# A windowed-attention and MLP kernel: the fallback path moved off VectorE, the guard's flag computed earlier, and the last tile's first store issued by SyncE

## The chip, the cores and the metric

The kernel runs on one core of a Trainium2 chip. The metric is the device time of one execution in microseconds, as the median of several runs; lower is better. One more execution is taken with the hardware profiler. Engines are named as the profile names them: PE (TensorE), PEld (its weight loads), DVE (VectorE), ACT (ScalarE), POOL (GpSimd), SP (SyncE). A q behind an engine's name (ACTq) marks what its sequencer does itself: waits, branches, register loads, DMA issues.

## The reference

Two stages: attention with four sink keys and a window of 128, then a normalised two-layer MLP with a residual.

```python
# q, k, v: (4, 8, 768, 64); n_sink = 4, window = 128
scores = (q @ k.T) / sqrt(64)
keep = (key < n_sink) | (0 <= query - key < window)
a = softmax(where(keep, scores, -1e9))         # the row maximum is taken off first
x = (a @ v).transpose(0, 2, 1, 3).reshape(4, 768, 512)
xn = (x - mean(x)) / sqrt(var(x) + 1e-6) * g_ln
out = x + maximum(xn @ w_ch1, 0) @ w_ch2       # 512 -> 2048 -> 512, float32
```

## The kernel before

The 4 x 768 rows are 24 tiles of 128 rows, taken in 12 chunks of two tiles. A chunk's q and k are brought into transposed layout (through PE for the first chunks, by transposing DMAs on SP for later ones), the scores of a key block against the query block are made in PSUM, ACT takes their exponential (L685, L740), DVE multiplies by a 0/1 mask (L744), and PE multiplies by v with a column of ones, so that the row sums come out beside the values (L774). DVE takes the reciprocal of the sums into the tile rec (L787), scales (L789) and makes the statistics (L793, L795, L797); POOL makes 1/sqrt(var) (L802, L803). The MLP of a chunk is 64 matmuls into four PSUM banks with ReLU by ACT (L843, L853), then 16 matmuls for each of its two tiles (L872), an add of the residual on DVE (L880) and a store of the tile (L884). The last tile's product is made in two halves of 256 columns, each with an add and a store of its own: the first half's store is issued by ACT, the second half's by SP.

The order is not written by hand. A planner (class Plan) gets every piece of work as P.op with an engine, a modelled cost and a due time, and simulates the engines; the instructions are then emitted in the order of the modelled start times. On PE, pieces with a due time above 40 are taken strictly by it. The MLP of chunk c is due from 16c + 8 on; the products of the last chunk's tiles have due times 192.5 to 195.5 in steps of one for the second last tile (four groups of four matmuls), and from 196.5 on for the last one.

The fast path leaves the row maximum out, which holds as long as no row sum leaves a wide range. A guard checks that: three DVE operations clamp rec, compare, and count the deviations into n_bad (L906 to L908); PE adds the count up over the partitions with one small float32 matmul (gsum, L911, due 196.2); DVE casts the result into the integer tile flag (L913). After all planned work every engine loads the flag into a register (L941), and each branches on it (L942): if it is above zero, the function general computes everything again with the row maximum taken off; otherwise each engine jumps over its part of that code to the end of the program. There SP waits for all DMA queues and all engines, and a barrier over the five engines ends the program (L977). With these inputs the flag is zero and general does not run.

general (L232 to L355) is a loop over the four batches with the six row blocks written out. Its softmax runs mainly on DVE: maxima, subtractions, sums, reciprocal, multiplications; so do the statistics and the last add.

Of the kernel before, what the change touches and what calls it, by code (L numbers as in the profile page):

```python
# [9 lines left out]
AF = mybir.ActivationFunctionType  # L10
ALU = mybir.AluOpType
# [186 lines left out]
def pe(us):  # L198
    return {"PE": (us, us + Plan.PE_DRAIN)}
# [26 lines left out]
NEVER = -1e9  # L226
# [5 lines left out]
def general(tc, nc, slots, pairs, ones, ident_f, ident, w1, w2, mhalf, g_s, g_r, q, k, v, out, scale):  # L232


    V, A, G, T, DMA = nc.vector, nc.scalar, nc.gpsimd, nc.tensor, nc.gpsimd.dma_start
    B, H, S, D = q.shape
    RB, HP, NS, DM = S // 128, H // 2, g_s.shape[2], H * D
    f32 = {n: [t.bitcast(FP32) for t in slots[n]] for n in ("kT", "qT", "kts", "pe")}
# [5 lines left out]
    sc = [t.rearrange("p a b c -> p (a b c)").rearrange("p (h c) -> p h c", h=4) for t in slots["natf"]]  # L244
    aT = [[flat(f32["pe"][2 * i + a]) for a in range(2)] for i in range(3)]
    xs, os_, xn, xnt, h1 = slots["ot"][0:2], slots["ot"][2:4], slots["xc"][0], slots["xnt"][0], slots["h1"]
    mx, sm = g_r[:, 0, :], g_r[:, 1, :]

    def transposes(src, dst):
# [4 lines left out]
    with tc.For_i(0, B, 1) as b:  # L254
# [5 lines left out]
        for r in range(RB):  # L260
            x, cur, prev = xs[r % 2], r % 2, (r + 1) % 2
# [4 lines left out]
            transposes(k_n, kT[cur])  # L266
            if r == 0:
                for t in sc:
                    V.memset(t[:, :, 0:128], NEVER)
            for a in range(HP):  # L270
                s_ps = pairs[a % 2]
                for h2 in range(2):
# [20 lines left out]
                if r < 2:  # L293
                    A.copy(sink, g_s[:, 4 * i:4 * i + 4, :])
            if r < 2:
                V.memset(g_s, NEVER)
            X = mybir.AxisListType.X
            V.tensor_reduce(out=mx, in_=g_s, op=ALU.max, axis=X)
            for i, t in enumerate(sc):
                V.tensor_reduce(out=g_r[:, 2, 4 * i:4 * i + 4], in_=t, op=ALU.max, axis=X)  # L300
            V.tensor_tensor(mx, mx, g_r[:, 2, :], op=ALU.max)
            for t, m in ((g_s, mx), (sc[0], mx[:, 0:4]), (sc[1], mx[:, 4:8])):
                V.tensor_tensor(t, t, m.unsqueeze(2).to_broadcast(list(t.shape)), op=ALU.subtract)
                A.activation(t, t, AF.Exp)
            V.tensor_reduce(out=sm, in_=g_s, op=ALU.add, axis=X)
            for i, t in enumerate(sc):
                V.tensor_reduce(out=g_r[:, 2, 4 * i:4 * i + 4], in_=t, op=ALU.add, axis=X)
            V.tensor_tensor(sm, sm, g_r[:, 2, :], op=ALU.add)
            V.tensor_scalar(sm, sm, 1e-9, None, op0=ALU.add)
            V.reciprocal(sm, sm)  # L310
            for t, m in ((g_s, sm), (sc[0], sm[:, 0:4]), (sc[1], sm[:, 4:8])):
                V.tensor_tensor(t, t, m.unsqueeze(2).to_broadcast(list(t.shape)), op=ALU.mult)
            for a in range(2):
                for i, rows in ((0, 128), (1, 128), (2, NS)):
                    for h in range(4):
# [11 lines left out]
                    T.matmul(ones[3][:, ds], lhsT=l, rhs=m, start=n == 0, stop=n == len(use) - 1)  # L327
            A.copy(x, ones[3])
            st = slots["st"][r % 2]
            V.bn_stats(st[:, 8:14], x)  # L330
            V.bn_aggr(st[:, 14:16], st[:, 8:14])
            G.tensor_scalar(st[:, 17:18], st[:, 15:16], 1e-6, None, op0=ALU.add)
            G.tensor_tensor(st[:, 16:17], st[:, 17:18], mhalf, op=ALU.pow)
            V.tensor_scalar(xn, x, st[:, 14:15], st[:, 16:17], op0=ALU.subtract, op1=ALU.mult)
            pb = ones[0].bitcast(BF16)
            for j in range(4):
                T.transpose(pb[:, 128 * j:128 * j + 128], xn[:, 128 * j:128 * j + 128], ident)
# [10 lines left out]
            for i in range(2):  # L348
                for ht in range(16):
                    at = 256 * (ht % 2) + 128 * i  # L350
                    T.matmul(ones[2 + i], lhsT=h1[ht // 2][:, at:at + 128], rhs=w2[ht // 4][:, ht % 4, :],
                             start=ht == 0, stop=ht == 15)
                V.tensor_tensor(os_[i], ones[2 + i], xs[i], op=ALU.add)
                at = 128 * (r - 1 + i)
                DMA(out[b, at:at + 128, :], os_[i])  # L355

# [2 lines left out]
def kernel(  # L359
# [12 lines left out]
    nc = tc.nc  # L372

    B, H, S, D = q.shape
    NS = int(n_sink)
# [3 lines left out]
    DM = moe_w_ch1.shape[0]  # L379
# [4 lines left out]
    NC = B * RC  # L384
# [7 lines left out]
    P = Plan()  # L392
# [6 lines left out]
    ones = [psum.tile([128, 512], FP32, name=f"one{i}") for i in range(4)]  # L399
# [31 lines left out]
    junk = const("junk", [128, 512], BF16)  # L431
    rec, low = const("rec", [128, NT, H], FP32), const("low", [128, NT, H], FP32)
    n_bad, flag = const("n_bad", [128, 1], FP32), const("flag", [1, 1], mybir.dt.int32)
    g_s, g_r = const("g_s", [128, H, NS], FP32), const("g_r", [128, 3, H], FP32)
    ones_f = const("ones_f", [128, 1], FP32)
    mhalf, one_e = const("mhalf", [128, 1], FP32), const("one_e", [128, 2], FP32)
# [10 lines left out]
    V, G = nc.vector, nc.gpsimd  # L447
# [377 lines left out]
    def mlp(c):  # L825
        T = 16.0 * c + 8.0
        xnt = xnt_b[c]
        h1 = []
        by_tile = c < PAR["by_tile"]
        for u in range(NH1 // 2):  # L830
            ph, hb = Buf(f"ph{c}_{u}", "one"), Buf(f"h{c}_{u}", "h1")

            def mm_t(e, u=u, ph=ph):
                for s in range(4):
                    for j in range(NDM):
                        nc.tensor.matmul(ph.t[:, 128 * s:128 * s + 128], lhsT=w1[u // 2][:, j, 128 * s:128 * s + 128],  # L836
                                         rhs=xnt.t[:, j, 128 * (u % 2):128 * (u % 2) + 128], start=j == 0, stop=j == NDM - 1)

            def mm(e, u=u, ph=ph):
                for s in range(2):  # L840
                    ht = 2 * u + s
                    for j in range(NDM):
                        nc.tensor.matmul(ph.t[:, 256 * s:256 * s + 256],  # L843
                                         lhsT=w1[ht // 4][:, j, 128 * (ht % 4):128 * (ht % 4 + 1)],
                                         rhs=xnt.t[:, j, :], start=j == 0, stop=j == NDM - 1)
            pr = T + u + 0.5
            o = P.op(f"ph{c}_{u}", pe(0.944 if by_tile else 0.872), pr, mm_t if by_tile else mm, reads=[xnt_t[2 * c + u % 2] if by_tile else xnt, (Bw1 if c < PAR["x_by_dma"] else Bw1g)[u // 2]],
                     writes=[ph], hold=[hb, xnt])
            last_use[u // 2] = [o]

            def rl(e, ph=ph, hb=hb):
                if e == "ACT":
                    nc.scalar.activation(hb.t, ph.t, AF.Relu)  # L853
                else:
                    V.tensor_scalar_max(hb.t, ph.t, 0.0)
            P.op(f"rl{c}_{u}", {"ACT": act(512), "DVE": dve(512)}, pr - 3, rl, reads=[ph], writes=[hb])
            h1.append(hb)
        T += 8
        for i in range(2):
            t = 2 * c + i  # L860
            b, r = t // RB, t % RB
            ot, st, rs, x = Buf(f"ot{t}", "ot"), xst_b[t], xst_b[t, "rs"], x_b[t]
            parts = 2 if t == NT - 1 else 1
            wd = DM // parts
            for f in range(parts):
                pc = Buf(f"pc{t}{f}", "one")
                sl = slice(wd * f, wd * (f + 1))
                for s in range(4):
                    def mm(e, s=s, i=i, pc=pc, sl=sl, wd=wd):
                        for ii in range(4):  # L870
                            ht = 4 * s + ii
                            nc.tensor.matmul(pc.t[:, 0:wd],  # L872
                                             lhsT=(h1[2 * s + i].t[:, 128 * ii:128 * ii + 128] if by_tile else
                                                   h1[ht // 2].t[:, 256 * (ht % 2) + 128 * i:256 * (ht % 2) + 128 * i + 128]),
                                             rhs=w2[s][:, ii, sl], start=ht == 0, stop=ht == NH1 - 1)
                    P.op(f"pc{t}{f}_{s}", pe(0.865 / parts), T + 4 * i + s + 2 * f + 0.5, mm,
                         reads=[*([h1[2 * s + i]] if by_tile else h1[2 * s:2 * s + 2]), Bw2[s]], **({"writes": [pc]} if s == 0 else {"rw": [pc]}))
                oo = Buf(f"oo{t}{f}")
                P.op(f"o{t}{f}", {"DVE": dve(wd, 1.14)}, T + 4 * i + 3.5, lambda e, sl=sl, pc=pc, wd=wd, ot=ot, st=st, x=x:
                     V.scalar_tensor_tensor(ot.t[:, sl], in0=pc.t[:, 0:wd], scalar=st.t[:, 16:17],  # L880
                                            in1=x.t[:, sl], op0=ALU.mult, op1=ALU.add),
                     reads=[pc, st, rs, x], writes=[ot, oo])
                P.op(f"st{t}{f}", {"ACT" if parts == 2 and not f else "SP": (0.35, 0.4)}, T + 4 * i + 3.6,
                     lambda e, sl=sl, ot=ot, b=b, r=r: (nc.sync if e == "SP" else nc.scalar).dma_start(  # L884
                         out[b, 128 * r:128 * (r + 1), sl], ot.t[:, sl]),
                     reads=[ot, oo], dma=HW_S)
# [18 lines left out]
    def guard(e):  # L905
# [2 lines left out]
        V.tensor_reduce(out=n_bad, in_=low, op=ALU.add, axis=mybir.AxisListType.XY)  # L908
    nb_b, pt_f, fl_b = Buf("n_bad"), Buf("ptf", "one"), Buf("flag")
    P.op("guard", {"DVE": fix(0.9)}, 1000.0, guard, reads=recs, writes=[nb_b])  # L910
    P.op("gsum", pe(0.06), 16.0 * NC + 4.2, lambda e: nc.tensor.matmul(  # L911
        pt_f.t[0:1, 0:1], lhsT=n_bad, rhs=ones_f, start=True, stop=True), reads=[nb_b, Bc["ones_f"]], writes=[pt_f])
    P.op("gflag", {"DVE": fix(0.1)}, 1000.0, lambda e: V.tensor_copy(flag, pt_f.t[0:1, 0:1]),  # L913
         reads=[pt_f], writes=[fl_b])
# [4 lines left out]
    t = 1.2  # L919
    for o in order:  # L920
# [5 lines left out]
        if n > 0 and o.start - t > 0.6:  # L926
            free = [(max([e_ for b_, e_ in banks[i].lives if b_ < t], default=0.0), i) for i in range(8)
                    if all(e_ < t or b_ > o.start + 0.3 for b_, e_ in banks[i].lives)]
            if free:
                i = min(free)[1]  # L930
# [51 lines left out]
```

## Time and profile before

| what | us |
|---|---|
| median of three runs (221.90, 222.38, 223.41) | 222.38 |
| the profiled execution's own time | 222.43 |
| its span, first to last instruction | 220.8 |
| PE busy / DVE busy / ACT busy / POOL busy | 212.1 / 117.2 / 108.8 / 89.8 |
| granted TensorE clock, mean | 0.998 |
| last matmul group begins, takes | 212.78, 3.61 |
| last add on DVE begins, takes | 216.49, 0.48 |

How to read it: the span counts from the first instruction of the profiled execution to the last; the execution's own time is 1.6 us longer, which lies around it. "Busy" leaves out waits, branches, register loads and DMA issues; these appear only as queue rows (ACTq and so on), with their duration in ns and the start of the first and last in us from the span's start. In the chain of waits a row is a start, a length and the work that held the end back. A TENSOR_LOAD is the load of the flag into an engine's register, a COMPARE_BRANCH the branch on it, an EVENT_SEMAPHORE a wait or a signal.

### The profile page before, as it was taken

The numbers are of one execution on the slowest core, as the hardware profiler recorded it, in microseconds if no ns is written. First come the engines' busy times: TensorE is split into PE (matmuls) and PEld (weight loads), VectorE is DVE, ScalarE is ACT, GpSimd is POOL, SyncE is SP. The second block draws the span as 40 slices with busy tenths as digits, with TensorE's granted clock in tenths as the row PEclk, the third lists the DMA queues.
The fourth block names the chain that finished last, engine by engine and source line by source line (L and its number), as shares of the span: only waits on it lengthen the run. The fifth ranks groups of instructions, "written<-read, shape, count | busy, mean of one in ns | idle before, by whom it ended". The sixth has DMA issues, their size and how long they took to land.

```text
span 220.8 us, 5072 instructions
## 1 busy us (share of the span) xinstructions
PE 212.1 (96%) x2033; PEld 144.6 (65%) x2033; DVE 117.2 (53%) x269; ACT 108.8 (49%) x163; POOL 89.8 (41%) x130
## 2 busy tenths in 40 slices
PE   6888999999999999999999999999999999999991
PEld 2556975764964964964955965965955955966861
DVE  5499745585796725725706815716706706722011
ACT  3767565145546447445546546445545546531700
POOL 7987663798073480760460741740110110120000
PEclk9999999999999999999999999999999999999999
DMA  5999999999999896999997997998713511111012
GB/s 158 160 184 206 177 207 193 155 211 149 175 171 141 137 146 110 149 127 119 143 124 119 143 118 121 130 123 111 129 38 80 136 28 47 59 39 72 23 52 62
DMA packets 108576, 27.45 MB, mean 124 GB/s; under 512 B 99201, under 2 KB 105601, under 8 KB 108545
## 3 DMA queue, kind: packets, MB, share of 16 engines
q0 software_dynamic: 74944, 13.11, 79.6%
q1 hardware_dynamic: 32400, 13.28, 29.4%
q10 hardware_dynamic: 1200, 0.66, 1.1%
q8 instruction: 18, 0.29, 0.6%
q14 instruction: 14, 0.11, 0.1%
HBM read 27.30 MB, written 6.29 MB: 152 GB/s over the span
## 4 chain that ended last, share of the span: by engine, by line
PE 90%; DVE 4%; DMA 2%; ACT 1%; issue 1%; DVEq 0%
PE one L872 39%; PE one L843 35%; PE pair L726 5%; PE pair L774 4%; PE one L836 2%; DMA natf<-in_k_dram 2%; PE pair L769 1%; DVE st L793 1%; DVE x L789 1%; PE one L632 1%; PE one L576 1%; PE one L730 1%; PE pair L665 1%; DVE xnt L821 1%; DVE xc L797 1%
## 5 line engine op out<-in xcount | busy, mean ns | idle before, releaser
L872 PE MATMUL one<-w,h 128*128 128x512 bf16 (+1 forms) x400 | 89.0, 371 | 0.0
L853 ACT ACTIVATE h<-one 128x512 bf16<-128x512 f32 x95 | 56.8, 598 | 59.3 <-PE one L843 54.2
L843 PE MATMUL one<-xnt,w 128*128 128x256 bf16 x704 | 82.4, 273 | 0.0
L843 PEld LDWEIGHTS <-w 128*128 128x128 bf16 x704 | 67.4, 98 | 10.2
L872 PEld LDWEIGHTS <-h 128*128 128x128 bf16 x400 | 37.4, 98 | 38.6 <-issue 2.0
L744 DVE TENSOR_TENSOR pe<-pe,mask 128x1024 bf16<-128x1024 bf16 (+1 forms) x40 | 26.0, 650 | 55.6 <-ACT pe L740 54.7
L740 ACT ACTIVATE pe<-pair 128x1024 bf16<-128x1024 f32 (+1 forms) x40 | 36.2, 957 | 34.1 <-PE pair L726 31.8
L618 POOL DMA_DIRECT2D nat<-in_k_dram x16 | 14.3, 893 | 39.6 <-DMA kT<-nat 29.7
L880 DVE SCALAR_TENSOR_TENSOR ot<-one,st,x 128x512 f32<-128x512 f32 (+1 forms) x25 | 18.2, 726 | 22.6 <-PE one L872 22.4
L802 POOL TENSOR_SCALAR st<-st 128x1 f32<-128x1 f32 x24 | 7.5, 313 | 43.2 <-DVE st L795 42.1
L541 POOL DMA_DIRECT2D vn<-in_v_dram x24 | 21.9, 920 | 3.7 <-DMA w<-in_moe_w_ch_dram 3.1
L618 POOL DMA_DIRECT2D nat<-in_q_dram x16 | 14.8, 926 | 11.7 <-DMA qT<-nat 8.5
L793 DVE BATCH_NORM_STATS2 st<-x 128x6 f32<-128x512 bf16 x24 | 16.7, 695 | 0.8
L774 PEld LDWEIGHTS <-pe 128*128 128x128 bf16 x352 | 14.0, 97 | 2.3 <-ACT pe L685 0.6
L803 POOL TENSOR_TENSOR st<-st,mhalf 128x1 f32<-128x1 f32 x24 | 14.2, 593 | 2.0
L789 DVE TENSOR_TENSOR x<-pair,rec 128x512 bf16<-128x512 f32 x20 | 13.8, 691 | 0.7
L726 PEld LDWEIGHTS <-kT 64*128 64x128 bf16 x216 | 6.9, 94 | 8.5 <-issue 8.3
L774 PE MATMUL pair<-vn,pe 128*128 128x65 bf16 x296 | 12.2, 193 | 0.0
L726 PE MATMUL pair<-qT,kT 64*128 64x128 bf16 (+1 forms) x216 | 11.6, 238 | 0.0
L797 DVE TENSOR_SCALAR xc<-x,st 128x512 bf16<-128x512 bf16 x24 | 9.1, 377 | 0.9
L787 DVE RECIPROCAL rec<-pair 128x8 f32<-128x8 f32 x20 | 4.1, 204 | 9.9 <-PE pair L774 9.9
L685 ACT ACTIVATE pe<-pair 128x1024 bf16<-128x1024 f32 (+1 forms) x8 | 7.2, 918 | 3.6 <-PE pair L679 3.6
(84 smaller groups left out, 123.3 us busy)
## 6 DMA issues: line engine op xcount, KB each, us to landing
out_dram<-ot SPq DMA_DIRECT2D x23, 256.0 KB
w<-in_moe_w_ch_dram POOLq DMA_DIRECT2D x8, 512.0 KB, 12.3
vn<-in_v_dram POOLq DMA_DIRECT2D x24, 128.0 KB, 6.1
nat<-in_k_dram POOLq DMA_DIRECT2D x22, 128.0 KB, 5.8
nat<-in_q_dram POOLq DMA_DIRECT2D x22, 128.0 KB, 5.0
natf<-in_k_dram SPq DMA_DIRECT2D x2, 256.0 KB
natf<-in_q_dram ACTq DMA_DIRECT2D x2, 256.0 KB
xnt<-xc SPq DMA_TRANSPOSE x18
```

The costliest lines, as they stand in the source:

```text
L541: P.op(f"vld{t}", {"POOL": (0.87, 0.9)}, prio, lambda e: G.dma_start(bv.t[:, :, 0:64], v[b, :, 128 * r:128 * (r + 1), :].rearrange("h p d ...
L618: lambda e, nat=nat, ap=ap: G.dma_start(nat.t, ap), writes=[nat], dma=SW)
L726: nc.tensor.matmul(pp.t[:, h2, col:col + q1 - q0], lhsT=kt.t[rs, hp, k0:k0 + 128], rhs=qT.t[rs, hp, q0:q1], start=i == 0, stop=True, skip_ ...
L740: P.op(f"ex{c}{hp}", {"ACT": act(2 * n)}, d + 0.1 + 0.05 * j, lambda e, pp=pp, pb=pb: nc.scalar.activation(pb.t[:, :, 0:n], pp.t[:, :, 0:n ...
L744: V.tensor_mul(pb.t[:, :, 0:n], pb.t[:, :, 0:n], mm),
L774: nc.tensor.matmul(bank(h // 4)[:, 65 * (h % 4):65 * (h % 4) + 65], lhsT=part(h, n), rhs=vn_b[tv].t[:, h, :], start=(not R and h % 4 == 0 ...
L789: P.op(f"x{t}{run[0]}", {"DVE": dve(512 * share)}, dd + 0.11, lambda e, pv=pv, rc=rc, run=run: V.tensor_tensor(x.t[:, 256 * run[0]:256 * r ...
L793: P.op(f"bn{t}", {"DVE": fix(0.60)}, d + 0.12, lambda e: V.bn_stats(st.t[:, 8:14], x.t), reads=[x], writes=[st, mv])
L843: nc.tensor.matmul(ph.t[:, 256 * s:256 * s + 256], lhsT=w1[ht // 4][:, j, 128 * (ht % 4):128 * (ht % 4 + 1)], rhs=xnt.t[:, j, :], start=j ...
L853: nc.scalar.activation(hb.t, ph.t, AF.Relu)
L872: nc.tensor.matmul(pc.t[:, 0:wd], lhsT=(h1[2 * s + i].t[:, 128 * ii:128 * ii + 128] if by_tile else h1[ht // 2].t[:, 256 * (ht % 2) + 128 ...
L880: V.scalar_tensor_tensor(ot.t[:, sl], in0=pc.t[:, 0:wd], scalar=st.t[:, 16:17], in1=x.t[:, sl], op0=ALU.mult, op1=ALU.add),
```

## The change

In general, DVE keeps the maxima and the reciprocal. Fills, subtractions, multiplications and the additions of the small sums go to POOL; the row sums and the statistics are made by ACT with an accumulating output, with POOL for the small steps; the last add becomes a copy by ACT and an add by POOL. In the planned part two things change: gsum is due at 192.7 instead of 196.2, and the first half's store of the last tile is issued by SP. All lines from L232 on are higher by up to six in the changed file.

By the built programs' instruction lists, three things move in the planned part. On PE the small matmul stands behind the first four of the second last tile's 16 matmuls instead of behind all 16. On DVE the cast of the flag stands ahead of that tile's add instead of behind it, with one wait instruction fewer. On SP the flag's load stands ahead of that tile's store, and both halves' stores are the last two before the branch; on ACT the flag's load follows the last activation directly. Behind the branch DVE has 34 rows instead of 128, ACT 185 instead of 155, POOL 168 instead of 92; PE and SP keep theirs.

```diff
@@ general
+    junk = f32["pe"][8].rearrange("p a b -> p (a b)")[:, 0:256]
...
-                    V.memset(t[:, :, 0:128], NEVER)
+                    G.memset(t[:, :, 0:128], NEVER)
...
-                V.memset(g_s, NEVER)
+                G.memset(g_s, NEVER)
...
-                V.tensor_tensor(t, t, m.unsqueeze(2).to_broadcast(list(t.shape)), op=ALU.subtract)
+                G.tensor_tensor(t, t, m.unsqueeze(2).to_broadcast(list(t.shape)), op=ALU.subtract)
                 A.activation(t, t, AF.Exp)
-            V.tensor_reduce(out=sm, in_=g_s, op=ALU.add, axis=X)
-            for i, t in enumerate(sc):
-                V.tensor_reduce(out=g_r[:, 2, 4 * i:4 * i + 4], in_=t, op=ALU.add, axis=X)
-            V.tensor_tensor(sm, sm, g_r[:, 2, :], op=ALU.add)
-            V.tensor_scalar(sm, sm, 1e-9, None, op0=ALU.add)
+            for h in range(H):
+                A.activation(junk, sc[h // 4][:, h % 4, :], AF.Copy, accum_out=sm[:, h:h + 1])
+            for n in range(NS):
+                G.tensor_tensor(sm, sm, g_s[:, :, n], op=ALU.add)
+            G.tensor_scalar(sm, sm, 1e-9, None, op0=ALU.add)
             V.reciprocal(sm, sm)
...
-            V.bn_stats(st[:, 8:14], x)
...
+            A.activation(os_[0], x, AF.Copy, accum_out=mean)
...
-                V.tensor_tensor(os_[i], ones[2 + i], xs[i], op=ALU.add)
+                A.copy(os_[i], ones[2 + i])
+                G.tensor_tensor(os_[i], os_[i], xs[i], op=ALU.add)
@@ the last tile's stores
-                P.op(f"st{t}{f}", {"ACT" if parts == 2 and not f else "SP": (0.35, 0.4)}, T + 4 * i + 3.6,
+                P.op(f"st{t}{f}", {"SP": (0.35, 0.4)}, T + 4 * i + 3.6,
@@ the guard
-    P.op("gsum", pe(0.06), 16.0 * NC + 4.2, lambda e: nc.tensor.matmul(
+    P.op("gsum", pe(0.06), 16.0 * NC + 0.7, lambda e: nc.tensor.matmul(
```

More of the change, by code (lines that the diff above doesn't have):

```diff
@@ L302, in general @@
             for t, m in ((g_s, mx), (sc[0], mx[:, 0:4]), (sc[1], mx[:, 4:8])):
-                V.tensor_tensor(t, t, m.unsqueeze(2).to_broadcast(list(t.shape)), op=ALU.subtract)
+                G.tensor_tensor(t, t, m.unsqueeze(2).to_broadcast(list(t.shape)), op=ALU.subtract)
                 A.activation(t, t, AF.Exp)
-            V.tensor_reduce(out=sm, in_=g_s, op=ALU.add, axis=X)
-            for i, t in enumerate(sc):
-                V.tensor_reduce(out=g_r[:, 2, 4 * i:4 * i + 4], in_=t, op=ALU.add, axis=X)
-            V.tensor_tensor(sm, sm, g_r[:, 2, :], op=ALU.add)
-            V.tensor_scalar(sm, sm, 1e-9, None, op0=ALU.add)
+            for h in range(H):
[3 more added lines that the diff above has]
+            G.tensor_scalar(sm, sm, 1e-9, None, op0=ALU.add)
             V.reciprocal(sm, sm)
             for t, m in ((g_s, sm), (sc[0], sm[:, 0:4]), (sc[1], sm[:, 4:8])):
-                V.tensor_tensor(t, t, m.unsqueeze(2).to_broadcast(list(t.shape)), op=ALU.mult)
+                G.tensor_tensor(t, t, m.unsqueeze(2).to_broadcast(list(t.shape)), op=ALU.mult)
             for a in range(2):
@@ L329, in general @@
             st = slots["st"][r % 2]
-            V.bn_stats(st[:, 8:14], x)
[L331 to L334, printed above, removed]
+            mean, var, rstd = st[:, 8:9], st[:, 9:10], st[:, 10:11]
+            A.activation(os_[0], x, AF.Copy, accum_out=mean)
+            G.tensor_scalar(mean, mean, 1.0 / DM, None, op0=ALU.mult)
+            G.tensor_scalar(os_[1], x, mean, None, op0=ALU.subtract)
+            A.activation(os_[0], os_[1], AF.Square, accum_out=var)
+            G.tensor_scalar(var, var, 1.0 / DM, 1e-6, op0=ALU.mult, op1=ALU.add)
+            G.tensor_tensor(rstd, var, mhalf, op=ALU.pow)
+            G.tensor_scalar(xn, os_[1], rstd, None, op0=ALU.mult)
             pb = ones[0].bitcast(BF16)
```

## The prediction

> **What bounds the kernel now.** I read the page first, then the chain that ended last, then the stretch behind the last matmul line by line.
>
> ```profile
> span 220.8 us, 5072 instructions
> PE 212.1 (96%) x2033; PEld 144.6 (65%) x2033; DVE 117.2 (53%) x269; ACT 108.8 (49%) x163; POOL 89.8 (41%) x130
> ```
>
> PE is busy for 96% of the span. An edit that neither takes a matmul away nor makes one wait can only act on what is left at the ends. The general path is behind a branch that these inputs don't take: the trace has 5072 instructions and none of its lines. So its rewrite can cost or save nothing but code: how far each engine jumps over it.
>
> ```profile
> 209.21 3.45 PE one L872 x16
> 212.66 0.12 PE one L911 x2
> 212.78 3.61 PE one L872 x32
> ...
> 216.49 0.48 DVE ot L880
> ```
>
> That is the end of the chain of waits: the second last output tile's product, the guard's sum, the last tile in two halves, the last add. It stops at 216.97, but the span ends at 220.85. What fills these 3.88 us is bookkeeping that only queue rows show. First, when each engine reads the flag (rows of the tile flag):
>
> ```profile
> L941 POOLq TENSOR_LOAD <-flag x1: 483/483/483, 213.6 to 213.6; - x1
> L941 SPq TENSOR_LOAD <-flag x1: 502/502/502, 213.9 to 213.9; - x1
> L941 PEldq TENSOR_LOAD <-flag x1: 765/765/765, 214.3 to 214.3; - x1
> L941 DVEq TENSOR_LOAD <-flag x1: 578/578/578, 216.5 to 216.5; - x1
> L941 ACTq TENSOR_LOAD <-flag x1: 475/475/475, 216.6 to 216.6; - x1
> ```
>
> ACT reads it last, though its last activation ends at 209.91. Ahead of its load stands the first half's store, which waits for the add that ends at 216.11:
>
> ```profile
> 216.14 0.37 ACTq L884 DMA_DIRECT2D out_dram<-ot  x1
> ...
> 217.00 0.34 SPq L884 DMA_DIRECT2D out_dram<-ot  x1
> ```
>
> Then the branch, and the first instruction behind it (rows of line 942):
>
> ```profile
> L942 PEldq COMPARE_BRANCH  x1: 3777/3777/3777, 215.1 to 215.1; - x1
> L942 ACTq COMPARE_BRANCH  x1: 54/54/54, 217.1 to 217.1; - x1
> L942 DVEq COMPARE_BRANCH  x1: 72/72/72, 217.2 to 217.2; - x1
> ...
> L942 DVEq EVENT_SEMAPHORE  x1: 21/21/21, 218.2 to 218.2; - x1
> L942 PEldq EVENT_SEMAPHORE  x1: 51/51/51, 219.0 to 219.0; - x1
> L942 ACTq EVENT_SEMAPHORE  x1: 17/17/17, 219.9 to 219.9; - x1
> ```
>
> From branch to next instruction ACT takes 2.76 us (217.10 to 219.87), POOL 2.64 (214.14 to 216.78), PE 3.83 (215.14 to 218.98), DVE 0.97, and SP 0.22, which jumps over few rows. The queue rows say why: behind three of the branches an instruction packet starts about 1.0 us later (PE 216.15, a 16 KB packet of 1.42 us; POOL 215.14, 0.45 us; ACT 218.03, 0.74 us), and the engine goes on 1.1 to 1.35 us after it ends.
>
> ```profile
> q8 instruction: 18, 0.29, 0.6%
> q14 instruction: 14, 0.11, 0.1%
> ```
>
> q8's 16 KB packets are PE's code, q14's 8 KB packets that of the others. Last, whom SP waits for before it lets the program end:
>
> ```profile
> SPq L977 <- ACTq L942: 0.8, 1, 0.8
> ...
> SPq L977 <- PEq L942: 0.4, 1, 0.4
> ```
>
> SP's waits are in order: PE is met at 219.04, the last store's landing at 219.54, ACT at 219.89. SP leaves at 219.95 and the rest is 0.90 us of barrier. So **ACT's late branch sets the end**.
>
> **The change part by part.**
>
> *General path.* Behind the branch DVE's rows fall from 128 to 34, ACT's rise from 155 to 185, POOL's from 92 to 168; PE and SP have as many as before. ACT and POOL jumped over enough to fetch already, so I cost them at 0 more. DVE jumps nearly as short as SP: 0.22 instead of 0.97, so it answers at 217.45 instead of 218.18. PE's 219.04 covers both. Without that cover it would be worth 0.75 at most. Value taken: 0.
>
> *Sum and flag sooner.* On PE the sum moves from behind the tile's 16 matmuls to behind the first four. Its price is the step in the cadence: L872's matmul at 212.283 would be followed at 212.499, the next began at 212.714, so 0.215 us, paid at either place: 0 net. What it reads is ready (n_bad ends at 194.80) and the bank was last read by the third-last relu (ends 208.16). So PE's end stays at 216.39. The fourth matmul starts at 209.69; the sum's signal came 0.51 behind the matmul before it, so now at 210.21; the cast of 0.136 starts at once on an idle DVE (9.69 us idle before the add at 212.76). The flag stands at 210.40 instead of 213.57. On DVE three adds are queued behind the cast, the first due at 212.7: 2.3 us of slack. The cast has one semaphore wait fewer, and DVE held the first half's add until 215.63 though its last wait ended at 215.23. I can't tell what these 0.40 us were: if they go, the half's store is 0.40 sooner and nothing waits for it; if they fall on the second half's add, that store is 0.40 later. I take 0, as the three full-tile adds behind 195 us start 0.045 after their wait.
>
> *SP's order.* SP now loads the flag ahead of the full tile's store. Load and checks take 0.83 us (213.92 to 214.74), so SP is free at about 211.2; that store is due at 213.53. Hidden by 2.3 us; if the flag came behind 212.7, the store would be late by the difference.
>
> *First half's store by SP.* ACT loses a DMA issue of 0.37 and its wait for 216.12. ACT then loads the flag at 210.43, branches at 210.98, answers at 213.74 instead of 219.87. SP issues the half at 216.14 (0.33 to 0.54, as its 24 stores took) and is free again by 216.68, before the last half's add signals at 216.98. Cost 0 on SP; queue q10 is left and q1 holds both halves.
>
> *What is late next.* The last store: 13 of its 16 parts landed by 218.70, the others at 219.06, 219.13 and 219.54. The last ran behind ACT's code packet (218.03 to 218.77, the store's packets there from 218.76 on): that packet is gone from this stretch. The one at 219.13 ran behind the first half's packets (till 218.32), which had run behind PE's code packet (216.15 to 217.57): that stays. So the store is down at about 219.13, PE at 219.04 as before, since PE's sequencer reaches its load at 214.27 only, when it has issued its matmuls, 0.7 after the old flag already.
>
> *Sum.* SP sees the store at 219.13 and leaves at 219.19 instead of 219.95: 0.76 less. General path 0, sum and flag 0 by themselves, order 0, store -0.76. The profiled execution took 222.43 with a span of 220.85, so 1.58 lies around it; it is 0.05 above the median 222.38. 222.38 - 0.76 = **221.6**, span 220.1.
>
> [...] Row: on the one engine the second half's first packet came at 218.324, right behind the first half's end mark at 218.318, though the two were on different queues. [...]
>
> **The rivals.**
>
> 1. *More goes than that.* PE's code packet took 1.42 us beside POOL's, DVE's and the first half's traffic; those at 193.73 and 211.04 took 0.92 and 0.96. With POOL's and ACT's fetches gone, PE answers 0.45 sooner (218.6), the first half's packets are not held, and the store is down at 218.7 to 218.75. SP leaves at 218.8: 1.15 less, 221.2. Against it: the first half's packets still fall there.
>
> 2. *The second half waits behind the first.* Eight packets of 0.046 each, 0.37 us on a held engine: landing 219.50, gain 0.39, 222.0. The 0.40 of the add, if it falls on the second half, gives nearly the same time.
>
> 3. *The change doesn't do what it says.* The flag is sooner, but no one on the path reads it sooner (PE reaches its load when it does), and the store lands at 219.5 behind another packet (one of q14 ran at 217.42 for 0.56, not surely DVE's). Then SP leaves at 219.6 to 219.95: 222.0 to 222.4.
>
> 4. *Slower.* SP's queue carries the second half only once the first is down. The first landed at 218.81; a store that wasn't held took 1.70 from issue to landing (217.00 to 218.70): 220.5, SP leaves 0.6 later than now: 223.0. It decides once the landing is past 219.89. Against it: two stores issued at 41.77 and 42.62 had their packets in flight together.
>
> **How the numbers follow.** Forecast (221.4 to 221.9) 0.50, more goes 0.20, half behind half 0.13, not what it says 0.11, slower 0.06. The range takes rivals 1 to 3 and some tenths on either side, as the three runs of before lie 1.5 us apart: 220.9 to 222.5. A measurement of this kernel can tell about 1% from no change, which is 2.2 us; no case reaches that, as the whole stretch from the last add to the end is 3.88 us and 1.7 of it is the store itself. What is left for over 1% is what I haven't seen: faster 0.03, within 1% 0.93, slower 0.04.
>
> **What would show it.** In the changed profile: the cast at about 210.3; ACT's load at 210.4 and its first instruction behind the branch near 213.7; POOL's near 213.6; DVE's gap at its branch 0.2 instead of 0.97; PE's load still at 214.3 and its answer at 218.6 to 219.0; SP's wait for ACT gone from the list of waits, with PE or the landing of the last store in its place; span near 220.1. I am wrong if PE's last matmul ends past 216.6 (the sum costs more there), if the last store is issued past 217.1, or if its landing is past 219.6.

## The result and the profile after

22 runs of the changed kernel have a median of 221.79 us (221.01 to 222.33), 22 runs of the kernel before, taken beside them, 222.76. The ratio is 0.9959, with a 95% interval of 0.9949 to 0.9970: about 0.4% faster, where 221.6 was forecast. The profiled execution took 221.36 with a span of 219.86, against 222.43 and 220.85.

Of the 0.99 us between the two spans, 0.33 is not the change's. In the profile of before the last matmul ends at 216.39, after at 216.06. Up to 28 us, among the first loads, casts and evictions, PE's starts in the two traces differ by up to 0.52; from there on the changed kernel is ahead by the same 0.34 in every matmul up to the last chunk. Over the profiled executions of this study the end of the last matmul varies from 215.98 to 217.05. So below everything is measured from the end of the last matmul, and the **tail**, from there to the end of the span, is the measure of a profile: **4.45 before, 3.80 after, 0.66 less** (before rounding) where 0.76 was forecast.

The page of after, and its chain of waits:

```profile
span 219.9 us, 5071 instructions
PE 212.3 (97%) x2033; PEld 144.7 (66%) x2033; DVE 118.1 (54%) x269; ACT 108.8 (49%) x163; POOL 89.5 (41%) x130
```

```profile
208.87 0.86 PE one L878 x4
209.73 0.12 PE one L917 x2
209.85 6.21 PE one L878 x44
...
216.15 0.48 DVE ot L886
```

PE does the same matmuls. The sum (L917) now stands behind four matmuls of the second last tile, and costs 0.12 there as it did behind sixteen. The cast of the flag starts at 209.89 instead of 213.42. Who reads it (rows of the tile flag):

```profile
L947 SPq TENSOR_LOAD <-flag x1: 461/461/461, 210.1 to 210.1; - x1
L947 ACTq TENSOR_LOAD <-flag x1: 463/463/463, 210.1 to 210.1; - x1
L947 POOLq TENSOR_LOAD <-flag x1: 487/487/487, 210.1 to 210.1; - x1
L947 PEldq TENSOR_LOAD <-flag x1: 753/753/753, 213.9 to 213.9; - x1
L947 DVEq TENSOR_LOAD <-flag x1: 541/541/541, 216.2 to 216.2; - x1
```

ACT, which read it last at 216.6, reads it at 210.1. PE and DVE read it no sooner measured from the last matmul, since their own work stands ahead. The branch, and the first instruction behind it (rows of line 948):

```profile
L948 ACTq COMPARE_BRANCH  x1: 50/50/50, 210.6 to 210.6; - x1
L948 ACTq EVENT_SEMAPHORE  x1: 17/17/17, 213.8 to 213.8; - x1
L948 PEldq COMPARE_BRANCH  x1: 3696/3696/3696, 214.8 to 214.8; - x1
L948 DVEq COMPARE_BRANCH  x1: 72/72/72, 216.8 to 216.8; - x1
L948 DVEq EVENT_SEMAPHORE  x1: 21/21/21, 217.0 to 217.0; - x1
L948 PEldq EVENT_SEMAPHORE  x1: 51/51/51, 218.5 to 218.5; - x1
```

ACT's jump of 3.2 us now lies beside PE's matmuls. DVE jumps in 0.23. And SP's list of waits in the last 12 us has no row for ACT any more:

```profile
SPq L947 <- DVE flag L919: 7.0, 1, 7.0
SPq L890 <- DVE ot L886: 4.1, 2, 2.5
SPq L890 <- DVEq L948: 1.2, 1, 1.2
SPq L983 <- PEq L983: 0.7, 2, 0.5
```

The third row is SP's wait ahead of the last issue. The profile puts it down to DVE's branch row, but the add that it waits for had ended at 216.63. The last store's last part lands at 218.88, SP leaves at 218.96, PE had answered at 218.55: the store ends the tail, as forecast. One row was not forecast, the issue of that store on SP, in the profile of after and then of before:

```profile
L890 SPq DMA_DIRECT2D out_dram<-ot x1: 842/842/842, 216.7 to 216.7; - x1
```

```profile
L884 ACTq DMA_DIRECT2D out_dram<-ot x1: 373/373/373, 216.1 to 216.1; - x1
L884 SPq DMA_DIRECT2D out_dram<-ot x1: 341/341/341, 217.0 to 217.0; - x1
```

SP needed 0.84 us for it instead of 0.34. The same in a table, in us from the end of the last matmul:

| event | before | after |
|---|---|---|
| first half's store issued | -0.25 (ACT) | -0.61 (SP) |
| second half's store issued, for | 0.60, 0.34 | 0.60, 0.84 |
| its 16 parts landed | 2.13 to 3.14 | 2.62 to 2.82 |
| PE, ACT, DVE, POOL go on behind the branch | 2.58, 3.47, 1.76, 0.39 | 2.49, -2.22, 0.97, -2.16 |
| SP leaves its waits | 3.56 | 2.90 |
| end of the span | 4.45 | 3.80 |

### The profile page after: what moved, and what is told of

Same layout as the page of the kernel before. It is cut to its first block, busy times and chain, and to the rows that moved or that the text cites. A ratio compares the mean times of both kernels' runs of the same rounds, so it can differ in the third digit from the quotient of the medians.

```text
span 219.9 us, 5071 instructions
## 1 busy us (share of the span) xinstructions
PE 212.3 (97%) x2033; PEld 144.7 (66%) x2033; DVE 118.1 (54%) x269; ACT 108.8 (49%) x163; POOL 89.5 (41%) x130
## 4 chain that ended last, share of the span: by engine, by line
PE 91%; DVE 4%; DMA 2%; ACT 1%; issue 1%; DVEq 0%
PE one L878 39%; PE one L849 35%; PE pair L732 5%; PE pair L780 4%; PE one L842 2%; DMA natf<-in_k_dram 2%; PE pair L775 1%; DVE st L799 1%; PE one L638 1%; DVE x L795 1%; PE one L582 1%; PE one L736 1%; PE pair L671 1%; DVE xnt L827 1%; PE one L816 0%
## 5 line engine op out<-in xcount | busy, mean ns | idle before, releaser
L808 POOL TENSOR_SCALAR st<-st 128x1 f32<-128x1 f32 x24 | 6.9, 289 | 42.5 <-DVE st L801 41.3
L809 POOL TENSOR_TENSOR st<-st,mhalf 128x1 f32<-128x1 f32 x24 | 14.8, 618 | 2.0
L803 DVE TENSOR_SCALAR xc<-x,st 128x512 bf16<-128x512 bf16 x24 | 9.6, 402 | 0.9
```

## The experiments

Three questions: which part of the change pays; what holds SP's issue; and what would be worth more. Where an expectation speaks of the stretch behind the last matmul, it is the tail. Each ratio is against the kernel before, run beside it.

### Which part pays

**The flag alone** (on the kernel before):

```diff
-    P.op("gsum", pe(0.06), 16.0 * NC + 4.2, ...
+    P.op("gsum", pe(0.06), 16.0 * NC + 0.7, ...
```

> The kernel before with only the guard's sum and flag moved forward; ACT still issues the first half's store. My theory (ACT's late branch sets the end): ACT reads the flag at once but only behind its store, so its branch stays 0.7 us behind the last matmul's end and the code fetch behind it stays; the stretch from the last matmul's end to the span's end stays at 4.4 to 4.5 us (before 4.46, after 3.79), ratio to before 0.999 to 1.001. Rival A (the sooner flag brings the gain): stretch 3.8, ratio 0.996 to 0.997.

Measured: 222.19 us, 0.9976 [0.9959, 0.9994]; tail 4.32. ACT reads the flag only behind its store. It branches at 0.36, sooner than the 0.7 expected because the first half's add ends 0.36 sooner here, and answers at 3.34: by the profile the early flag alone is worth 0.13. The tail and the ratio both lie outside the ranges expected. The median fell by 0.5; the interval reaches down to 0.1, and no row of the tail shows the rest.

**The store alone** (on the kernel before):

```diff
-  {"ACT" if parts == 2 and not f else "SP": (0.35, 0.4)}
+  {"SP": (0.35, 0.4)}
```

> The kernel before with only the first half's store moved from ACT to SP; the flag comes as late as before. My theory: ACT reads the flag at 213.6, branches at 214.1 and answers at 216.9, ahead of PE's 218.5 to 219.0, so nearly all of the gain is there: stretch from the last matmul's end to the span's end 3.7 to 4.0 us, ratio 0.996 to 0.998. DVE still jumps 128 rows and answers 1 us behind its branch, which is covered. Rival A (the flag) and rival B (DVE's short jump): stretch 4.4 to 4.5, ratio 1.000. If SP's issue of the second half takes 0.84 instead of 0.34 us here too, it belongs to the two stores on one queue and not to the flag or the general path.

Measured: 222.07, 0.9975 [0.9958, 0.9993]; tail 3.91. ACT reads the late flag as soon as it is there, branches at -2.28 and answers at 0.20:

```profile
L942 ACTq COMPARE_BRANCH  x1: 50/50/50, 214.3 to 214.3; - x1
L942 ACTq EVENT_SEMAPHORE  x1: 17/17/17, 216.8 to 216.8; - x1
```

So freeing ACT from the store is most of the gain in the tail, 0.54 of 0.66. SP's second issue takes 0.958 here:

```profile
L884 SPq DMA_DIRECT2D out_dram<-ot x1: 958/958/958, 217.2 to 217.2; - x1
```

**The rewritten fallback alone** (general of the changed kernel, the rest of before):

> The kernel before with only the general path rewritten. Rival B (the gain is DVE's jump, 0.23 instead of 0.97 us, about the size of the gain measured): stretch 3.7 to 3.9, ratio 0.996 to 0.997. My theory: DVE answers 0.75 sooner and nobody waits for it: stretch 4.4 to 4.5, ratio 0.999 to 1.001.

Measured: 222.69, 1.0001 [0.9983, 1.0020]; tail 4.69, ended by ACT, which answers at 3.71, as its jump took 3.00 in this profile. That is 0.24 more than before and above the range expected. DVE does jump in 0.23 instead of 0.97, and it is worth nothing:

```profile
L948 DVEq COMPARE_BRANCH  x1: 72/72/72, 217.2 to 217.2; - x1
L948 DVEq EVENT_SEMAPHORE  x1: 21/21/21, 217.4 to 217.4; - x1
```

**Flag and store, with the old fallback:**

> The changed kernel with the general path as it was before. My theory: stretch as after, 3.7 to 3.9 us, ratio 0.995 to 0.997; DVE answers at 1.8 us behind the last matmul's end instead of 1.0, still ahead of the last store's landing at 2.8. Rival B: at least 0.5 of the gain is missing, stretch 4.3 to 4.5.

Measured: 221.56, 0.9955 [0.9937, 0.9973]; tail 3.94, second issue 0.891, landing 2.96. By the medians the whole gain is there without the rewrite. Of the tail's 0.66 it has 0.51; its 3.94 lies just above the range expected. Its store lands 0.14 later than in the changed kernel, behind a longer issue (0.891 instead of 0.842) and a longer code packet (1.37 instead of 1.29). As the rewrite alone did not shorten the tail, the 0.14 is not put down to it.

### What holds SP's second issue

The theory (C, where a letter is given), a guess from the rows of after: the first half's packets stand in SP's own queue, the last of them held behind PE's 16 KB code packet (it ran from -0.22 to 1.06; 15 of the half's parts were down by 1.60, the last at 2.23), and SP cannot finish the next issue into that queue until they move. Rivals: SP issues slower because it did so just before, or any store is slow there.

**One store for the whole tile** (on after; both adds first, then all 512 columns):

```diff
+                if f < parts - 1:
+                    continue
+                sl = slice(0, DM)
```

> The changed kernel with one store of the last tile's 512 columns behind both adds instead of two of 256. Theory C (SP's second issue took 0.84 us because the first half's packets stood in the same queue, held behind PE's code packet): with nothing ahead of it the issue takes 0.33, its packets start 0.84 behind its start, and the landing comes about 0.2 to 0.3 sooner or, as the store is twice as large (a full tile took 2.0 from issue to last landing, a half 1.7), at about the same time; stretch from the last matmul's end to the span's end 3.5 to 3.8 us (after 3.79), ratio to before 0.995 to 0.997. Rival D (the long issue comes from SP's own code or its place in the program): the issue stays at 0.8 and the stretch grows to 4.1 us.

Measured: 221.54, 0.9952 [0.9939, 0.9965]; tail 3.65. With nothing ahead of it in the queue the issue takes 0.332, and twice the bytes land at 2.43 to 2.61:

```profile
L893 SPq DMA_DIRECT2D out_dram<-ot x1: 332/332/332, 217.5 to 217.5; - x1
```

**The halves further apart** (on after: the second half's products of the last tile are due two later, so more of them stand behind the first half's, and that half's store is issued at -1.04 instead of -0.61):

```diff
-  T + 4 * i + s + 2 * f + 0.5, mm,
+  T + 4 * i + s + 4 * f + 0.5, mm,
```

> The changed kernel with the first half's 16 matmuls all ahead of the second half's instead of mixed: the first half's product ends 1.75 us ahead of the last matmul's end instead of 1.31, so its store is issued about 0.45 sooner, and most of its packets are through before PE's code packet starts (0.2 ahead of the last matmul's end). Theory C: the first half lands sooner, SP's second issue falls to 0.34 to 0.6, the store lands 0.1 to 0.4 sooner and PE's answer, 2.5 behind the last matmul's end, is next: stretch 3.4 to 3.7 us, ratio 0.994 to 0.996. If the first half's packets still meet the code packet, nothing changes: 3.8.

Measured: 222.07, 0.9972 [0.9957, 0.9987]; tail 3.69. Both halves are on SP, the issue takes 0.332, and the first part lands at 2.12 instead of 2.62. So issuing two halves does not make SP slow by itself. The ratio missed its range (0.994 to 0.996). PE's code packet ran from 0.18 to 1.14 here, and held the first half's last part till 2.31 all the same.

That last point speaks against the theory as it is worded: a part of the first half was held here as well, and SP's issue was not. What differs is the order. Here the first half's packets begin at -0.21, ahead of the code packet at 0.18. In the three kernels with a long issue (after, the store alone, flag and store) the code packet began first, at -0.22 to -0.25, and the half's packets at 0.23 to 0.59. So the issue is long where the code packet gets ahead of the half's packets; what SP waits for there is open.

The long issue is not special to the tail. In mid-run one store of a full tile took 0.924 to issue in this kernel, and one 1.430 in the kernel with a single store. Each had transposing DMAs ahead of it in SP's queue, and each ended 0.38 behind the end of a 16 KB packet of PE (at 73.80 and 74.68).

**First half by ACT, with ACT's part of the fallback left out,** so that ACT's jump is short (on after; the fallback then lacks all of ACT's work; it is not run):

```diff
-    V, A, G, T, DMA = nc.vector, nc.scalar, ...
+    V, A, G, T, DMA = nc.vector, Nothing(), ...
-  {"SP": (0.35, 0.4)}
+  {"ACT" if parts == 2 and not f else "SP": (0.35, 0.4)}
```

> The changed kernel with the first half's store back on ACT, and with ACT's part of the general path left out, so that ACT jumps over 9 rows; that path does not run with these inputs. PE's code fetch stays. Theory C: the two halves are on two queues again, so SP's second issue takes 0.33 to 0.37 us instead of 0.84 although the first half's packets still meet PE's code packet; the last store lands 2.3 to 2.75 behind the last matmul's end. ACT answers at about 0.8 although its branch is behind its store, so a late ACT branch costs only through the code fetch. Stretch from the last matmul's end to the span's end 3.5 to 3.7 us. If the issue stays at 0.8, theory C falls.

Measured: 224.43, 1.0088 [1.0070, 1.0106]; tail 6.52 where 3.5 to 3.7 was expected, and slower than before. Two queues: the issue takes 0.332 and the store lands at 2.31, as the theory has it. But PE, whose part was not touched, answers at 218.67 and then stands still until 222.10; SP's waits and PE's rows at the barrier:

```profile
SPq L988 <- PEq L988: 3.9, 2, 3.4
```

```profile
L953 PEldq EVENT_SEMAPHORE  x1: 51/51/51, 218.7 to 218.7; - x1
L988 PEldq DRAIN  x2: 8/8/8, 222.1 to 222.4; - x2
```

In the profiles of before and after 0.15 us lie between these two. A second 16 KB code packet starts at 219.29 and takes 1.33. Such a second packet comes in every kernel with PE's full fallback (after: at 219.26, for 1.27); only here does PE stand still past its end, which is at 220.62. With ACT's instructions left out, PE's waits for them go as well, so PE's code is shorter and its jump target moves. The next run asks whether it had come to stand at the end of what one 16 KB packet brings, there called a code block (theory E, where a letter is given; a guess from the second packet).

**The same, with 16 instructions put into PE's part of the fallback** (they are never run; they move the target on):

```diff
+    for _ in range(16):
+        T.transpose(ones[0][:, 0:128], ident_f, ident_f)
```

> The kernel of the run before last but two (first half's store on ACT, ACT's part of the general path left out) with 16 more matmuls in PE's part of the general path, which doesn't run; they only move the place that PE jumps to by 16 instructions or more. There PE stood still for 3.4 us between its first and its second instruction behind the branch, while a second 16 KB code packet came. Theory E: the place it jumps to lies at the end of a 16 KB code block, and PE needs the next block at once; moved, the wait is gone: stretch from the last matmul's end to the span's end 3.2 to 3.5 us instead of 6.5, ratio to the kernel before 0.993 to 0.996. Rival: the wait comes from ACT's missing code or the barrier; then it stays at 6.5.

Measured: 221.79, 0.9971 [0.9954, 0.9989]; tail 3.29, as expected, though the ratio is above its range (0.993 to 0.996). The 3.4 us are gone:

```profile
SPq L990 <- PEq L990: 0.7, 2, 0.5
```

The second half's issue takes 0.332 and it lands at 2.31, as in the run before. So the wait went when PE's target was moved. That it lay at a block's end stays a guess: no row shows where a block ends.

### What would be worth more, and what the order of the stores is worth

**A short fallback:** only the first of the six row blocks is left in general (it would leave five blocks of rows undone; it is not run), on after and then on before:

```diff
-        for r in range(RB):
+        for r in range(1):
```

> The changed kernel whose general path is cut to the first of its six row blocks, so that every engine jumps over few rows; with these inputs that path does not run. Theory: no engine fetches code behind its branch, PE answers within 0.3 us of it instead of 3.75, the first half's packets are held by nothing, SP's second issue takes 0.34 and its store lands 1.7 behind its issue, 2.3 behind the last matmul's end: stretch 3.2 to 3.4 us, ratio 0.993 to 0.995. If the 0.84 us issue stays (rival D), stretch 3.7 to 3.8.

Measured on after: 221.57, 0.9953 [0.9940, 0.9966]; tail 3.28. PE's branch takes 0.23 instead of 3.70 us, its packet is gone from the tail, and the store is issued in 0.332 and down at 2.31:

```profile
L948 PEldq COMPARE_BRANCH  x1: 228/228/228, 215.5 to 215.5; - x1
```

The median gains less than the tail does. In this profile the last matmul ends at 216.71, 0.32 later than before, and PE is that late from 21 us on. (The chain of waits begins only at the last add in this profile and the next, at 216.80 and 216.76. Counted from there the tails would be 3.19 and 3.21, and a later expectation quotes the 3.19. The add starts 0.1 behind the last matmul here as it does everywhere.)

> The kernel before with the general path cut to one row block in the same way; the flag is late and ACT still issues the first half's store. If what ACT paid was the code fetch behind a late branch, ACT's answer comes 0.2 to 0.4 behind its branch (before 2.76), and the end is set by the last store alone: stretch 3.1 to 3.4 us instead of 4.46, ratio 0.993 to 0.996. If it was the store on ACT's queue or the late flag as such, the stretch stays above 4.2.

Measured on before: 221.56, 0.9955 [0.9942, 0.9967]; tail 3.30. The flag is as late as ever (213.70) and ACT still issues the first half, yet ACT goes on 0.19 behind its branch:

```profile
L942 ACTq COMPARE_BRANCH  x1: 54/54/54, 217.4 to 217.4; - x1
L942 ACTq EVENT_SEMAPHORE  x1: 17/17/17, 217.6 to 217.6; - x1
```

So here a late branch cost next to nothing, those 0.19 us, with a near target. With a short jump, flag and store may stay as they were.

**PE's part of the fallback alone left out** (on after; the fallback then lacks all of PE's work; it is not run):

```diff
-    V, A, G, T, DMA = nc.vector, nc.scalar, nc.gpsimd, nc.tensor, ...
+    V, A, G, T, DMA = nc.vector, nc.scalar, nc.gpsimd, Nothing(), ...
```

> The changed kernel with PE's part of the general path left out, so that only PE's jump is short; that path does not run with these inputs. Theory C: without PE's 16 KB packet the first half is down at 1.0 to 1.4 behind the last matmul's end, SP's second issue takes 0.33, its store lands at 2.2 to 2.4, and the stretch is 3.1 to 3.35 us, as with the whole general path cut (3.19): what was left of the jump's cost is PE's alone. If DVE's, ACT's or POOL's code matters too, 3.5 or more.

Measured: 221.35, 0.9936 [0.9917, 0.9955]; tail 3.28, issue 0.333, first half down at 1.39 and second at 2.30. So what the far jumps still cost the changed kernel, 0.52 of its tail, is all PE's: with every jump short the tail was 3.28 as well.

**The halves' queues exchanged** (on after: first half by SP, second by ACT):

```diff
-  {"SP": (0.35, 0.4)}
+  {"ACT" if parts == 2 and f else "SP": (0.35, 0.4)}
```

> The changed kernel with the halves' issuers swapped: SP issues the first half, ACT the second. Theory (an engine's branch sets the end when it stands behind a late store): ACT loads the flag at about 1.0 behind the last matmul's end, branches at 1.5 and answers at 4.2 to 4.4; the stretch grows to 5.1 to 5.3 us against 3.80 after and 4.46 before, ratio to the kernel before 1.002 to 1.005. If ACT's branch is not what sets the end, the stretch stays below 4.2.

Measured: 223.28, 1.0030 [1.0017, 1.0043]; tail 5.10. The two stores are again on two queues, but ACT branches at 1.57 and answers at 4.11, and SP waits for it:

```profile
L948 ACTq COMPARE_BRANCH  x1: 54/54/54, 218.2 to 218.2; - x1
L948 ACTq EVENT_SEMAPHORE  x1: 17/17/17, 220.8 to 220.8; - x1
```

```profile
SPq L983 <- ACTq L948: 1.8, 1, 1.8
```

That is the cause of the gain with its sign turned: what the kernel pays for is when ACT gets to its branch.

No version that keeps the whole fallback beats the changed kernel: the single store (0.9952) and the old fallback (0.9955) lie within its interval. In one profile each, the tails of the single store (3.65) and of the halves apart (3.69) are a little shorter than its 3.80.

## Why the prediction was right, point by point

- **What bounds the end.** Right. ACT's late branch ended the tail before: it goes when ACT is freed (store alone, tail 3.91), comes back when ACT is loaded again (exchanged, 5.10), and stays when the fallback alone is rewritten (4.69).
- **General path, 0.** Right: 1.0001. DVE answers 0.23 behind its branch, 0.22 was forecast. The longer code of ACT and POOL costs nothing here, as both now jump beside PE's matmuls (they go on at -2.22 and -2.16).
- **Sum and flag.** Right. The sum is 0.12 at either place; the cast came at 209.89, or 210.22 with the 0.33 of the start put back, for a forecast 210.21 to 210.3; ACT answered at 213.84 and POOL at 213.90, or 214.17 and 214.23 with the 0.33, for a forecast 213.74 and 213.6: their jumps took 3.2 to 3.3 us, 0.5 to 0.6 longer than those of before, with nobody waiting for them. Of the 0.40 us by which DVE held the first half's add, the bound "they go" came true: that add ends at -0.64 in the kernel with the early flag alone, and at -0.28 in those with the store or the fallback alone. In the changed kernel nobody waits for it. What it was stays open.
- **SP's order, 0.** Right in that nothing came of it. The second last tile's store was issued at 213.42, or 213.75 with the 0.33, for a forecast 213.53: the sum's 0.215 now lies ahead of that tile's end, which the prediction did not count. Nobody waits for it.
- **First half's store by SP, "Cost 0 on SP".** This step failed, by 0.50 us: the second issue took 0.84. It is the second rival, half behind half, at another place: the price was paid in the issue and not on the wire. The row weighed in the prediction was about packets of two queues on one DMA engine; what one queue does to its issuer it could not show. Among the last stores the issue is long only where both halves are on SP and PE's code packet begins ahead of the first half's packets: 0.842, 0.958 and 0.891, each ending 0.37 to 0.44 behind the end of that packet. It is 0.33 to 0.35 where SP issues the second half and the first stands on ACT's queue, where nothing is ahead, where the packet is gone (0.333 and 0.332), and where the first half is issued 0.43 sooner and its packets begin first. Whether the second half stood strictly behind the first on every DMA engine, no row shows; the trace of after shows that all its parts landed (2.62 to 2.82) after the first's last (2.23). Why the issuer is held, no row shows either.
- **What is late next.** Right in kind, 0.08 off in size, but by another path: the last landing, at 2.82 for a forecast 2.74, then PE at 2.49. The forecast had 13 of the store's 16 parts down by 2.31 and the last one held behind the first half and PE's packet. In fact all 16 started late, behind the long issue, and landed within 0.20 us. The two come out near each other, as both were counted from the end of the same code packet: the held part landed 1.56 behind it in the profile of before, the last part here 1.75. The forecast's own path shows with the halves further apart: a short issue, 15 parts down by 2.30 and the last, held, at 2.71. So the 0.50 us of the issue cost about 0.1 at the landing.
- **The sum, 0.76.** The tail gave 0.66, and the missing 0.10 is the landing's 0.08 and 0.02 between it and SP's leaving. The medians differ by 0.97, and the interval of the ratio is 0.67 to 1.14 us; whether anything outside the tail adds to it is open, since the end of the last matmul scatters over 1.07 us. Kernels with equal tails differ in their medians, too: PE's part left out has 3.28 and 0.9936, the padded kernel 3.29 and 0.9971. That 221.79 lies near the forecast 221.6 is in part chance: from 222.76, the median measured beside it, the forecast saving leads to 222.0. And the measurement tells more than the prediction allowed it: its interval is 0.2% wide, where 1% was said to be the least that shows.
- **The rivals.** "More goes than that" asked for PE's packet to be faster: it took 1.29 instead of 1.42, and PE answered at 2.49 instead of 2.58, so its conditions came true only in small part. Its price, 1.15, lies just above the interval of 0.67 to 1.14 and 0.76 within it; it is the profile that tells the two apart. "Not what it says" fell with ACT's answer. "Slower" asked for 1.70 from the first half's landing to the second's: it was 0.59 (2.23 to 2.82).

## What to carry to other kernels

The branch over code that never runs cost each engine a jump of its own here (before, from 0.22 us on SP to 3.83 on PE), and SP left its waits only behind the last of them (before, ACT went on at 3.47, SP left at 3.56): find the engine that reaches its branch last, and take out of its queue what it waits for ahead of it (here one DMA issue, 0.54 of the tail). Where the jump itself was made short, that was worth more than any order around it (tail 3.3 instead of 3.8, PE's branch 0.23 instead of 3.70), and the place to look is the engine with the longest branch row, here PE; loops in the fallback in place of written-out blocks would be the way to try, which was not tried here. And read an effect of tenths of a microsecond from the stretch it acts on, not from medians: the end of the last matmul alone lay between 215.98 and 217.05 here.

## What the runs showed of the hardware

- **A far jump.** ACT and POOL go on 2.5 to 3.3 us behind a branch over the full fallback, and 0.2 to 0.5 behind one with a near target; PE's branch row is 3.4 to 3.9 us long for the one, and 0.23 to 0.24 for the other. Inside a far jump of PE lies an instruction packet: after, its branch begins at 214.79, a 16 KB packet runs from 215.84 to 217.12, and PE goes on at 218.55. The queues of such packets on the page of after:

```profile
q8 instruction: 18, 0.29, 0.6%
q14 instruction: 12, 0.10, 0.1%
```

  0.29 MB in 18 packets is 16 KB each, 0.10 MB in 12 is 8 KB. With PE's part of the fallback left out, q8 has 16 instead of 18: its packets are taken for PE's.

- **Where a jump's target lay cost as much as the jump.** PE stood still for 3.43 us one instruction behind its target, with a branch row of 3.47, in a kernel whose edit was on ACT and SP; 16 instructions that are never run took it away. That the target lay at the end of a code block is the author's guess, and is not shown.
- **Stores land late beside code packets.** A 16 KB packet took 1.0 to 1.4 us in the tails, and the last of a store's 16 parts landed late beside it: the first half was down at 1.4 to 1.5 without PE's packet in the tail, and at 2.0 to 2.4 with it.
- **An issue can be long beside a code packet.** SP's issue of a store took 0.84 to 1.43 us instead of 0.33 to 0.54 in five places of these traces, and each time it ended 0.37 to 0.44 behind the end of a 16 KB packet of PE.
